# Eight attention units with output products of 32 columns and other PSUM banks, ahead of a two-layer product

## The chip, the cores and the metric

The kernel runs on one core of one Trainium2 chip. The metric is the device time of one execution in microseconds (us), the median of several runs. TensorE is called PE below, VectorE DVE, ScalarE ACT, GpSimd POOL; SP is the engine that issues all DMAs here. PSUM, the memory that PE writes to, has eight banks.

## The reference

```python
# q, k, v: (4, 8, 768, 64); mem_k, mem_v: (4, 8, 8, 64); chunk 32, left 16, right 8
for c in range(24):
    k_full = concat(mem_k, k[c*32 - 16 : c*32 + 40])      # clipped at both ends; v_full alike
    scores = q_c @ k_full.T / 8
    a = exp(scores - max); a = a / (sum(a) + 1e-9)
    out[c] = a @ v_full
x = out, as (3072 tokens, 512)
h = x @ w_in                                               # w_in (512, 2048)
g = max(h, 0) + alpha * min(h, 0)
result = g @ w_out                                         # w_out (2048, 512)
```

The weights w_in and w_out arrive as 8-byte floating point numbers and are turned into 4-byte ones on the chip ("decoded").

## The kernel before

The 3072 tokens make 8 blocks of 384. A block's attention is 4 units, each a pair of heads; unit u belongs to block u // 4. The two-layer product goes over 16 slices f of the hidden width: for block and slice, `up` forms h (12 products of 128x384), `sides` its two Relu (ACT, L581), `join` their sum with alpha (DVE), `high` and `low` split it in two parts, and `down` (9 products of 128x512) adds it onto the block's output in three banks o0 to o2 (L603). Such a step is written (block, f).

The first eight units (blocks 0 and 1) are computed by `windows`, before and among the first slices, while the weights still arrive. A unit u has these steps on PE, called s, t and v here, each with the unit's number behind it: s, 12 score products (L269), ahead of which 2 products of `busy` (8 for the first unit) go into the same bank; t, one such product and 3 transposes of the weights of attention (L435); v, 24 output products (L450). Between s and t DVE and ACT form the weights of attention (L407 to L428). Between t and v ACT copies the transposes to `et` (L440). After v `split` forms xh (ACT, L376) and xl (DVE, L380), the input of `up`. The scores of all eight units use bank s0, the transposes s1, the outputs bank a. Block 1's down products of the first nine slices use the same three banks s0, s1 and a; block 0's use o0 to o2.

The order of work is not that of the code. `Plan` collects steps with an engine, an estimated cost, what they read and write (names such as ("s", 0) stand for a bank), and a rank `rest`. `send` then goes through time by these estimates and lets each engine take, of the steps that could begin, the one with the most work behind it, or the highest `rest`. A step that writes a name waits for all that was planned before with that name. Each engine carries out its list in that order. SP too works its list in order, so a load that waits for its buffer holds up those behind it. The loads of values for units 4 to 7 (`vw`, L395) take over the buffers of units 0 to 3, and so wait for the v steps of those.

A matmul on 4-byte numbers (scores, outputs) shows in the profile as two matmul and two weight load records, one on the rounded numbers of `up` and `down` as one of each.

Of the kernel before, what the change touches and what calls it, by code (L numbers as in the profile page):

```python
# [9 lines left out]
F32 = mybir.dt.float32  # L10
# [8 lines left out]
P = 128  # L19
B, H, S, D = 4, 8, 768, 64  # L20
NM = 8
CH, LEFT, RIGHT = 32, 16, 8
# [12 lines left out]
NTT = BT // P  # L35
# [24 lines left out]
PE, DVE, ACT, POOL, SP = "PE", "DVE", "ACT", "POOL", "SP"  # L60
# [27 lines left out]
NWIN, NSET = 2 * NPAIR, 4  # L88
# [64 lines left out]
def body(ctx: ExitStack, tc: tile.TileContext, qvw, kw, vw, w_in, w_out, alpha, out):  # L153
# [15 lines left out]
    ps_o = ctx.enter_context(tc.tile_pool(name="ps_o", bufs=1, space=bass.MemoryType.PSUM))  # L169
    ps_s = ctx.enter_context(tc.tile_pool(name="ps_s", bufs=1, space=bass.MemoryType.PSUM))  # L170
    ps_a = ctx.enter_context(tc.tile_pool(name="ps_a", bufs=1, space=bass.MemoryType.PSUM))
# [12 lines left out]
    vws = [turned.tile([P, NT * NJ, D], F32, name=f"vw{i}", tag=f"pt{i}") for i in range(NPT)]  # L184
# [14 lines left out]
    step = plan.add  # L199
    state, xs = {}, {}  # L200

    def rest(place):
        return (len(ORDER) - place) * PAIR
# [8 lines left out]
    def due(u, later=0):  # L212

        return rest(begins(u) + later)
# [41 lines left out]
    def score_products(u):  # L256
        blk, pr = divmod(u, NPAIR)
        st = state[u]
        k = u % 2 if u >= NWIN else 0
        s_ps = ps_s.tile([P, 512], F32, name="s_ps", tag=f"s{k}")  # L260
        if u < NWIN:
            stir(s_ps, STIR[0] if u == 0 else STIR[1])
        st["s"] = s_ps[:, :NJ * 2 * KW].rearrange("p (n h k) -> p n h k", n=NJ, h=2)
        st["sg"] = s_ps[:, :NJ * 2 * KW].rearrange("p (n k) -> p n k", k=KW)
        for n in range(NJ):
            for g in range(4):
                t, j = SLOT[(g, n)]
                c = t * NJ + j
                nc.tensor.matmul(  # L269
                    out=st["s"][g * CH:(g + 1) * CH, n],  # L270
                    lhsT=qs[sets(u)][:, c * CH:(c + 1) * CH],
                    rhs=kbs[sets(u)][:, :, t, STARTS[j]:STARTS[j] + KW],
                    start=True, stop=True,
                )
# [90 lines left out]
             rest=due(u, DUE_VALUES))  # L365
        split(u)

    def split(u):

        st = state[u]  # L370

        slot = u % NX

        def high():
            st["xh"] = xp.tile([P, BT], F32R, name="xh", tag=f"xh{slot}")
            nc.scalar.copy(out=st["xh"], in_=st["a"][:, :BT])  # L376

        def low():
            xl = xp.tile([P, BT], F32R, name="xl", tag=f"xl{slot}")
            nc.vector.tensor_tensor(out=xl, in0=st["a"][:, :BT], in1=st["xh"].bitcast(F32), op=ALU.subtract)  # L380
            xs[u] = (st["xh"], xl)

        xh, xl = ("xh", slot), ("xl", slot)
        step(ACT, 0.48, high, reads=["a"], writes=[xh])
        step(DVE, 0.56, low, reads=["a", xh], writes=[xl])

    def vw_keys(u):
        i = u % NSET
        return [("pt", i, j) for j in range(len(TURNS))] if i < NPT else [("vw", i)]
# [9 lines left out]
    def windows(u):  # L399

        st = state[u]
        sk, tk = ("s", 0), ("s", 1)

        def top():
            hide(u)
            st["mx"] = sm.tile([P, NJ * 2, 1], F32, name="mx", tag=f"mx{u % 3}")
            nc.vector.tensor_reduce(out=st["mx"], in_=st["sg"], axis=AX.X, op=ALU.max)  # L407

        def less():
            st["e"] = at.tile([P, NJ * 2, KW], F32, name="e", tag=f"e{u % 2}")  # L410
            nc.vector.tensor_tensor(out=st["e"], in0=st["sg"], in1=st["mx"].broadcast_to([P, NJ * 2, KW]),  # L411
                                    op=ALU.subtract)

        def exps():
            nc.scalar.activation(out=st["e"], in_=st["e"], func=AF.Exp, scale=SCALE)

        def total():
            st["den"] = sm.tile([P, NJ * 2, 1], F32, name="den", tag=f"den{u % 3}")
            nc.vector.tensor_reduce(out=st["den"], in_=st["e"], axis=AX.X, op=ALU.add)

        def guard():
            nc.vector.tensor_scalar(out=st["den"], in0=st["den"], scalar1=1e-9, scalar2=None, op0=ALU.add)

        def inverse():
            nc.vector.reciprocal(out=st["den"], in_=st["den"])

        def scale():
            nc.vector.tensor_tensor(out=st["e"], in0=st["e"], in1=st["den"].broadcast_to([P, NJ * 2, KW]),  # L428
                                    op=ALU.mult)

        def turn():
            st["t"] = ps_s.tile([P, 512], F32, name="t_ps", tag="s1")
            stir(st["t"], STIR[2])
            for n in range(NJ):
                nc.tensor.transpose(st["t"][:, n * P:(n + 1) * P],  # L435
                                    st["e"][:, 2 * n:2 * n + 2].rearrange("p h k -> p (h k)"), eye)

        def keep():
            st["et"] = turned.tile([P, NJ, P], F32, name="et", tag="e2")
            nc.scalar.copy(out=st["et"].rearrange("p n q -> p (n q)"), in_=st["t"][:, :NJ * P])  # L440

        def values():
            st["a"] = ps_a.tile([P, 512], F32, name="a_ps", tag="a")
            for n in range(NJ):
                for g in range(4):
                    t, j = SLOT[(g, n)]
                    c = t * NJ + j
                    for h2 in range(2):
                        rows = slice(h2 * D, (h2 + 1) * D)
                        nc.tensor.matmul(  # L450
                            out=st["a"][rows, c * CH:(c + 1) * CH],
                            lhsT=vws[u % NSET][rows, c, :],
                            rhs=st["et"][rows, n, g * CH:(g + 1) * CH],
                            start=True, stop=True,
                        )

        step(PE, 0.82 + (0.44 if u < NWIN else 0), partial(score_products, u), reads=[("q", sets(u)), ("k", sets(u), 0), ("k", sets(u), 1)],
             writes=[sk], rest=due(u))
        step(DVE, 0.66, top, writes=[sk, ("mx", u % 3)])
        step(DVE, 0.52, less, reads=[sk, ("mx", u % 3)], writes=e_keys(u))  # L460
        step(ACT, 0.52, exps, writes=e_keys(u))
        step(DVE, 0.56, total, reads=e_keys(u), writes=den_keys(u))
        step(DVE, 0.16, guard, writes=den_keys(u))
        step(DVE, 0.19, inverse, writes=den_keys(u))
        step(DVE, 0.55, scale, reads=den_keys(u), writes=e_keys(u))
        step(PE, 0.68, turn, reads=e_keys(u) + ["eye"], writes=[tk], rest=due(u, 1))
        step(ACT, 0.48, keep, reads=[tk], writes=["e2"])
        step(PE, 1.55, values, reads=["e2"] + vw_keys(u), writes=["a"], rest=due(u, 1))
        split(u)

    def zero():

# [85 lines left out]
    def hidden(blk, f, first_f, last_f):  # L558
# [3 lines left out]
        place = PLACE[blk, f]  # L562
# [53 lines left out]
                     writes=[hk], rest=rest(place))  # L616

        def add_bend():
            step(ACT, 0.98, sides, reads=[hk], writes=[sd])
            step(DVE, 0.61, join, reads=["nal"], writes=[sd])  # L620
            step(*((ACT, 0.51) if place < HIGH_ACT else (DVE, 0.35)), high, reads=[sd], writes=[gh])
            step(DVE, 0.56, low, reads=[sd, gh], writes=[gl])

        def add_down(o_ps):
            step(PE, 2.09, partial(down, o_ps), reads=[("w", 1, f, 0), ("w", 1, f, 1), gh, gl],
                 writes=[("s", 0), ("s", 1), "a"] if joint else ["o"],
                 rest=rest(place + 1.5))

        return add_up, add_bend, add_down
# [13 lines left out]
    def store(blk, o_ps):  # L643
        def copy(tt, t, o):
            if blk == 1:
                o["t"] = kept[tt]
                nc.vector.tensor_tensor(out=o["t"], in0=o_ps[tt], in1=o["t"], op=ALU.add)
            else:
                o["t"] = tmp.tile([P, DM], F32, name="o_t", tag=f"o{t}")
                nc.scalar.copy(out=o["t"], in_=o_ps[tt])  # L650

        def send(tt, o):
            r = blk * BT + tt * P
            nc.sync.dma_start(out=out[r:r + P, :], in_=o["t"])

        for tt in range(NTT):
            t = tt if blk == 1 else NTT + tt % 2 if blk == 0 else next(ntmp) % NTMP
            o = {}
            place = PLACE[blk, NF - 1] + 1
            step(DVE if blk == 1 else ACT, 0.68 if blk == 1 else 0.59, partial(copy, tt, t, o), reads=["o"],  # L660
                 writes=[("tmp", t)], rest=rest(place))
            step(SP, 0.75, partial(send, tt, o), reads=[("tmp", t)])

# [115 lines left out]
```

## Time and profile before

| | |
|---|---|
| three runs | 629.96, 632.6 and 633.72 us, median 632.6 |
| profiled execution | 630.4 us, with a span from first to last instruction of 628.3 us |
| granted PE clock | 0.994 on average |
| PE, its weight loads, DVE, ACT, POOL busy | 615.9, 537.7, 402.7, 259.4, 25.7 us |
| moved by DMA | 48.43 MB in 22,596 packets |

Read it as three stretches. Up to about 50 us the units of blocks 0 and 1 are computed; DMA is full from 10 to 70 us (a share near 1.0), and the weights arrive. Until about 130 us weights are decoded on DVE and ACT beside the first slices. After that come blocks 2 to 7, with PE busy without a break until the last 4 us. All times of the trace count from the span's start.

### The profile page before, as it was taken

How to read it: one execution, taken by the hardware profiler on the slowest of the kernel's cores; microseconds unless marked ns; L12 is line 12 of the kernel's file. 1: busy time of each engine (PE TensorE's matmuls, PEld its weight loads, DVE VectorE, ACT ScalarE, POOL GpSimd, SP SyncE). 2: the span in 40 equal slices, each digit the busy share in tenths (PEclk: the TensorE clock that was granted, in tenths of full speed). 3: DMA queues.
4: the chain of work that ended last, by engine and by line, in shares of the span. 5: the costliest groups of instructions: out<-in, count | busy, mean ns of one | idle time of the engine just before them, and what ended most of it. 6: DMA issues, size and time to landing. Idle time of an engine off the chain costs nothing.

```text
span 628.3 us, 10982 instructions
## 1 busy us (share of the span) xinstructions
PE 615.9 (98%) x4278; PEld 537.7 (86%) x4278; DVE 402.7 (64%) x984; ACT 259.4 (41%) x716; POOL 25.7 (4%) x37
## 2 busy tenths in 40 slices
PE   6998999999999999999999999999999999999997
PEld 3687999988888889888888888898888888988996
DVE  6778898978747666477465765467563784633332
ACT  2387888765424243442324423144133433231212
POOL 1001000001000000000000000001000010000000
PEclk9898999999999999999999999999999999999999
DMA  8999700023222020320105001040012100010001
GB/s 236 301 404 409 245 1 2 0 62 97 66 62 68 21 69 23 98 79 2 47 18 158 18 18 36 30 142 18 18 49 79 50 18 18 18 51 1 1 1 50
DMA packets 22596, 48.43 MB, mean 77 GB/s; under 512 B 3088, under 2 KB 7184, under 8 KB 22544
## 3 DMA queue, kind: packets, MB, share of 16 engines
q1 hardware_dynamic: 22544, 47.73, 23.8%
q8 instruction: 33, 0.54, 0.4%
q14 instruction: 19, 0.16, 0.1%
HBM read 41.43 MB, written 6.29 MB: 76 GB/s over the span
## 4 chain that ended last, share of the span: by engine, by line
PE 93%; DMA 5%; SPq 1%; DVE 0%; ACT 0%; issue 0%
PE o_ps L603 43%; PE h_ps L571 42%; DMA w_t<-w_out 4%; PE s_ps L269 4%; PE a_ps L357 3%; PE a_ps L450 1%; DMA kb<-kw 1%; SPq L235 0%; PE s_ps L254 0%; DVE mx L407 0%; DVE e L411 0%; PE t_ps L435 0%; PE t_ps L254 0%; ACT o_t L650 0%; ACT dn L581 0%
## 5 line engine op out<-in xcount | busy, mean ns | idle before, releaser
L571 PE MATMUL h_ps<-xh,w 128*128 128x384 f32 x1024 | 262.6, 337 | 0.0
L603 PE MATMUL o_ps<-w,gh 128*128 128x512 f32 x768 | 239.8, 393 | 0.0
L571 PEld LDWEIGHTS h_ps<-xh,w 128*128 128x128 f32 x1024 | 186.8, 189 | 3.8
L571 PE MATMUL h_ps<-xl,w 128*128 128x384 f32 x512 | 174.7, 341 | 2.3 <-DVE xl L380 1.4
L581 ACT ACTIVATE up<-h_ps 128x384 f32<-128x384 f32 x128 | 63.4, 495 | 260.2 <-PE h_ps L571 253.3
L603 PEld LDWEIGHTS o_ps<-w,gh 128*128 128x128 f32 x768 | 144.1, 188 | 27.9
L603 PE MATMUL o_ps<-w,gl 128*128 128x512 f32 x384 | 153.1, 399 | 0.0
L585 DVE SCALAR_TENSOR_TENSOR up<-dn,nal,up 128x384 f32<-128x384 f32 x128 | 79.7, 627 | 113.3 <-ACT dn L581 112.5
L341 DVE STREAM_TRANSPOSE pt<-e 32x192 f32<-32x192 f32 (+1 forms) x336 | 99.5, 301 | 10.2 <-POOL e L320 4.6
L571 PEld LDWEIGHTS h_ps<-xl,w 128*128 128x128 f32 x512 | 96.7, 189 | 8.5 <-DVE xl L380 1.5
L603 PEld LDWEIGHTS o_ps<-w,gl 128*128 128x128 f32 x384 | 72.1, 188 | 16.9 <-issue 2.6
L595 DVE TENSOR_TENSOR gl<-up,gh 128x384 fp32r<-128x384 f32 x128 | 70.8, 557 | 3.2 <-ACT gh L591 0.5
L581 ACT ACTIVATE dn<-h_ps 128x384 f32<-128x384 f32 x128 | 62.3, 487 | 0.0
L299 ACT ACTIVATE e<-s_ps,mx 128x64 f32<-128x64 f32 x144 | 43.5, 323 | 29.3 <-DVE mx L293 28.4
L591 DVE CAST gh<-up 128x384 fp32r<-128x384 f32 x104 | 36.4, 355 | 20.5 <-PE o_ps L603 17.1
L320 POOL TENSOR_TENSOR e<-e,den 128x384 f32<-128x384 f32 x24 | 21.1, 878 | 465.4 <-DVE den L317 346.0
L299 ACT ACTIVATION_READ_ACCUMULATOR e<-s_ps,mx 128x1 f32 x144 | 30.7, 213 | 0.0
L376 ACT CAST xh<-a_ps 128x384 fp32r<-128x384 f32 x32 | 15.4, 481 | 34.3 <-PE a_ps L357 26.2
L269 PEld LDWEIGHTS s_ps<-kb,q 128*32 128x32 f32 x672 | 17.2, 111 | 8.1 <-issue 7.2
L269 PE MATMUL s_ps<-kb,q 128*32 128x128 f32 x672 | 23.6, 279 | 0.5 <-DMA kb<-kw 0.5
L357 PEld LDWEIGHTS a_ps<-pt,v_t 128*64 128x64 f32 x384 | 16.6, 136 | 7.4 <-issue 7.4
L357 PE MATMUL a_ps<-pt,v_t 128*64 128x96 f32 x384 | 21.1, 252 | 0.0
(59 smaller groups left out, 294.2 us busy)
## 6 DMA issues: line engine op xcount, KB each, us to landing
w_t<-w_in SPq DMA_DIRECT2D x16, 512.0 KB, 9.9
w_t<-w_out SPq DMA_DIRECT2D x16, 512.0 KB, 10.1
kb<-kw SPq DMA_DIRECT2D x56, 136.0 KB, 2.8
v_t<-qvw SPq DMA_DIRECT2D x24, 256.0 KB, 2.7
out<-o_t SPq DMA_DIRECT2D x24, 256.0 KB, 2.7
q<-qvw SPq DMA_DIRECT2D x28, 192.0 KB, 2.5
vw<-vw SPq DMA_DIRECT2D x4, 384.0 KB, 6.3
early<-vw SPq DMA_DIRECT2D x4, 384.0 KB, 7.1
```

What stands on the lines that cost most here:

```text
L269: nc.tensor.matmul(out=st["s"][g * CH:(g + 1) * CH, n], lhsT=qs[sets(u)][:, c * CH:(c + 1) * CH], rhs=kbs[sets(u)][:, :, t, STARTS[j]:STAR ...
L299: nc.scalar.activation(out=st["e"][:, i], in_=st["sg"][:, i], func=AF.Exp, scale=SCALE, bias=st["mx"][:, i:i + 1], accum_out=st["den"][:, i])
L320: nc.gpsimd.tensor_tensor(out=st["e"], in0=st["e"], in1=st["den"].broadcast_to([P, NJ * 2, KW]), op=ALU.mult)
L341: nc.vector.transpose(out=pts[u % NPT][quad * CH:(quad + 1) * CH, j, t0:t0 + n1 - n0].rearrange("p t h q -> p (t h) q"), in_=(st["e"], zer ...
L357: nc.tensor.matmul(out=st["a"][h2 * D:(h2 + 1) * D, t * TQ:(t + 1) * TQ], lhsT=st["v"][:, t, h2, :], rhs=pts[u % NPT][:, :, t, h2, :], sta ...
L376: nc.scalar.copy(out=st["xh"], in_=st["a"][:, :BT])
L571: nc.tensor.matmul(out=h["ps"][:, :BT], lhsT=ws[f, 0][:, wk, k * P:(k + 1) * P], rhs=xs[first + k][xk], start=(k == 0 and n == 0), stop=(k ...
L581: nc.scalar.activation(out=h[name], in_=h["ps"][:, :BT], func=AF.Relu, scale=sign)
L585: nc.vector.scalar_tensor_tensor(out=h["g"], in0=h["dn"], scalar=nal[:, f:f + 1], in1=h["up"], op0=ALU.mult, op1=ALU.add)
L591: copy(out=h["gh"], in_=h["g"])
L595: nc.vector.tensor_tensor(out=h["gl"], in0=h["g"], in1=h["gh"].bitcast(F32), op=ALU.subtract)
L603: nc.tensor.matmul(out=o_ps[tt], lhsT=h[gk][:, tt * P:(tt + 1) * P], rhs=ws[f, 1][:, wk], start=(f == first_f and i == 0), stop=(f == last ...
```

## The change

- A unit's 24 output products become 48: each gave 64 columns of the stationary operand, two of 32 columns now give the same output, placed on four strips of PSUM partitions, taken in the order strip 0, 2, 1, 3.
- The scores of the first eight units go in turn into s0 and s1. The transposes go into o0, the outputs into o1 and o2 in turn. So bank a is used by them no more, and the first down product of block 0 has to wait for the last unit's split. For this the planner's one name "o" becomes three.
- The planner's cost for the output products is 0.95 in place of 1.55.
- `sides` (the Relu) gets the rank of its up products.

```diff
     def score_products(u):
-        k = u % 2 if u >= NWIN else 0
+        k = u % 2
...
-    def split(u):
+    def split(u, ak="a"):
...
-        step(ACT, 0.48, high, reads=["a"], writes=[xh])
-        step(DVE, 0.56, low, reads=["a", xh], writes=[xl])
+        step(ACT, 0.48, high, reads=[ak], writes=[xh])
+        step(DVE, 0.56, low, reads=[ak, xh], writes=[xl])
...
     def windows(u):
-        sk, tk = ("s", 0), ("s", 1)
+        sk, tk, ak = ("s", u % 2), ("o", 0), ("o", 1 + u % 2)
...
-            st["t"] = ps_s.tile([P, 512], F32, name="t_ps", tag="s1")
+            st["t"] = ps_o.tile([P, 512], F32, name="t_ps", tag="o0")
...
-            st["a"] = ps_a.tile([P, 512], F32, name="a_ps", tag="a")
+            st["a"] = ps_o.tile([P, 512], F32, name="a_ps", tag=f"o{1 + u % 2}")
...
-                    for h2 in range(2):
+                    for h2, i in ((0, 0), (1, 0), (0, 1), (1, 1)):
                         rows = slice(h2 * D, (h2 + 1) * D)
                         nc.tensor.matmul(
-                            out=st["a"][rows, c * CH:(c + 1) * CH],
-                            lhsT=vws[u % NSET][rows, c, :],
+                            out=st["a"][h2 * D + i * CH:h2 * D + (i + 1) * CH, c * CH:(c + 1) * CH],
+                            lhsT=vws[u % NSET][rows, c, i * CH:(i + 1) * CH],
                             rhs=st["et"][rows, n, g * CH:(g + 1) * CH],
...
-        step(PE, 1.55, values, reads=["e2"] + vw_keys(u), writes=["a"], rest=due(u, 1))
-        split(u)
+        step(PE, 0.95, values, reads=["e2"] + vw_keys(u), writes=[ak], rest=due(u, 1))
+        split(u, ak)
...
-            step(ACT, 0.98, sides, reads=[hk], writes=[sd])
+            step(ACT, 0.98, sides, reads=[hk], writes=[sd], rest=rest(place))
...
-                 writes=[("s", 0), ("s", 1), "a"] if joint else ["o"],
+                 writes=[("s", 0), ("s", 1), "a"] if joint else [("o", tt) for tt in range(NTT)],
```

The instructions move on several engines. First PE, from the output products of unit 0 (`a_ps` with `vw_161`) on; `busy` rows are the products into a bank ahead of its use. Before:

```order
L450 MATMUL a_ps<-et,vw_161 64x32 x24
L254 LDWEIGHTS busy
L254 MATMUL t_ps<-busy 128x512
L435 MATMUL t_ps<-eye,e 128x128 x3
L254 LDWEIGHTS busy
L254 MATMUL s_ps<-busy 128x512
L254 LDWEIGHTS busy
L254 MATMUL s_ps<-busy 128x512
L269 MATMUL s_ps<-early 32x128 x12
L450 MATMUL a_ps<-et,vw_162 64x32 x24
```

and now:

```order
L450 MATMUL a_ps<-et,vw_161 32x32 x48
L254 LDWEIGHTS busy
L254 MATMUL t_ps<-busy 128x512
L435 MATMUL t_ps<-eye,e 128x128 x3
L450 MATMUL a_ps<-et,vw_162 32x32 x48
L254 LDWEIGHTS busy
L254 MATMUL s_ps<-busy 128x512
L254 LDWEIGHTS busy
L254 MATMUL s_ps<-busy 128x512
L269 MATMUL s_ps<-kb_154,q_159 32x128 x12
```

The scores of unit 3 (`early`) stood between t1 and v1; they now come ahead of t0, and v1 follows its transposes at once, ahead of the scores of unit 4. The order of the change is s0, s1, s2, s3, t0, v0, t1, v1, s4, t2, v2, s5, t3, v3, three up products' groups of (0, 0), s6, t4, s7, the last group of (0, 0), v4, t5, v5, three groups of (0, 1), t6, the last group of (0, 1), one of (1, 0), v6, t7, one of (1, 0), v7, where a group is three products.

Second PE, around the output products of unit 7 (`a_ps` with `early`) and the first down products (`o_ps`). Before:

```order
L571 MATMUL h_ps<-xh,w 128x384 x2
L603 MATMUL o_ps<-w,gl 128x512
L603 MATMUL o_ps<-w,gh 128x512 x2
L603 MATMUL o_ps<-w,gl 128x512
L603 MATMUL o_ps<-w,gh 128x512 x2
L603 MATMUL o_ps<-w,gl 128x512
L603 MATMUL o_ps<-w,gh 128x512 x2
L450 MATMUL a_ps<-et,early 64x32 x24
L571 MATMUL h_ps<-xl,w 128x384
```

and now:

```order
L571 MATMUL h_ps<-xh,w 128x384 x2
L450 MATMUL a_ps<-et,early 32x32 x48
L571 MATMUL h_ps<-xl,w 128x384
L571 MATMUL h_ps<-xh,w 128x384 x2
L571 MATMUL h_ps<-xl,w 128x384
L571 MATMUL h_ps<-xh,w 128x384 x2
L603 MATMUL o_ps<-w,gl 128x512
L603 MATMUL o_ps<-w,gh 128x512 x2
```

The nine down products of (0, 0) went ahead of v7; they now come after it, and after the last two groups of up products of (1, 0).

Third ACT, around the Relu of (1, 0) (`up`, `dn`) and the last step of decoding two weights (`w`). Before:

```order
L376 CAST xh<-a_ps 128x384
L537 CAST w<-a 128x512
L537 CAST w<-a 128x2x512
L581 ACTIVATE up<-h_ps 128x384
L581 ACTIVATE dn<-h_ps 128x384
L591 CAST gh<-up 128x384
```

and now:

```order
L521 COPY w_t<-w_t 128x512
L581 ACTIVATE up<-h_ps 128x384
L581 ACTIVATE dn<-h_ps 128x384
L537 CAST w<-a 128x2x512
L537 CAST w<-a 128x512
L591 CAST gh<-up 128x384 x2
```

Those two weights stood ahead of the Relu and now come behind it.

More of the change, by code (lines that the diff above doesn't have):

```diff
@@ L659, in store @@
             place = PLACE[blk, NF - 1] + 1
-            step(DVE if blk == 1 else ACT, 0.68 if blk == 1 else 0.59, partial(copy, tt, t, o), reads=["o"],
+            step(DVE if blk == 1 else ACT, 0.68 if blk == 1 else 0.59, partial(copy, tt, t, o), reads=[("o", i) for i in range(NTT)],
                  writes=[("tmp", t)], rest=rest(place))
```

## The prediction

> **What bounds the kernel now.** I read the page first, then busy time by stretch, then the waits of TensorE (PE).
>
> ```profile
> span 628.3 us, 10982 instructions
> ...
> PE 615.9 (98%) x4278; PEld 537.7 (86%) x4278; DVE 402.7 (64%) x984; ACT 259.4 (41%) x716; POOL 25.7 (4%) x37
> ...
> q8 instruction: 33, 0.54, 0.4%
> ```
>
> ```profile
> 0.00:50.57 50.57, 41.82 (x675) 30.83 (x675) 37.82 (x92) 25.86 (x47) 4.67 (x13) 0.97 0.99 320
> 50.57:628.30 577.73, 574.11 (x3603) 506.87 (x3603) 364.90 (x893) 233.59 (x670) 21.06 (x24) 1.00 0.18 56
> 600.00:628.30 28.30, 24.68 (x122) 21.75 (x120) 9.23 (x18) 6.73 (x15) 0.00 (x0) 0.98 0.08 28
> ```
>
> Columns: stretch, its length, then busy time and count of PE, its weight loads, DVE, ACT, POOL; granted clock; DMA share; GB/s. From 50.57 PE idles only in the 3.6 us of the end. So the end is 50.57 plus the PE work then left. The change adds nothing after the opening. It is worth what it does to the time at which PE becomes dense, and to what has been done by then.
>
> ```profile
> PE s_ps L254 <- DVE e L411: 2.9, 2, 1.4
> PE s_ps L254 <- DVE busy L176: 1.5, 1, 1.5
> PE h_ps L571 <- DVE xl L380: 1.4, 1, 1.4
> PE a_ps L450 <- issue: 1.0, 1, 1.0
> PE h_ps L571 <- ACT dn L581: 1.0, 1, 1.0
> PE a_ps L450 <- ACT et L440: 0.6, 1, 0.6
> PE s_ps L269 <- DMA kb<-kw: 0.5, 1, 0.5
> ```
>
> Of these 8.9 us the change aims at 2.9 (one bank for scores) and 1.0 (Relu late). The fourth line I take to be the one that decides. In PE's timeline:
>
> ```profile
> 23.72 0.88 PE L450 MATMUL a_ps<-et,early 64*64 64x32 f32 x23
> 25.60 0.94 PE L450 MATMUL a_ps<-et,early 64*64 64x32 f32 x25 [1.00 <-issue]
> ```
>
> One group of 48 output products stops after 23 and goes on 1.0 us later, with no wait inside the group. PE's instructions come in by queue q8: 33 packets of 16 KB for 2 x 4278 matmuls and loads, 259 each. Since 33 packets carry nearly the whole program, little of it is held ahead. Below, the stretches end where one of these packets starts, but for the second, which ends at the stall; then two answers on the packets themselves, each for 0.02 us that holds the start of one, at 22.89 and at 31.04.
>
> ```profile
> 0.00:22.89 22.89, 17.54 (x298) 11.11 (x298) 15.48 (x41) 7.37 (x15) 2.89 (x10) 1.00 0.93 265
> 0.00:25.50 25.50, 19.25 (x345) 12.47 (x345) 18.05 (x49) 8.34 (x16) 2.89 (x10) 1.00 0.94 264
> 25.50:31.04 5.54, 5.44 (x93) 3.95 (x95) 3.52 (x9) 1.95 (x4) 0.00 (x0) 0.69 1.06 281
> 31.04:37.07 6.03, 6.03 (x107) 5.08 (x104) 4.79 (x15) 4.57 (x8) 0.00 (x0) 1.00 1.03 401
> 37.07:43.04 5.97, 5.90 (x75) 5.24 (x74) 5.97 (x14) 4.49 (x8) 0.00 (x0) 1.00 1.03 408
> 43.04:63.27 20.23, 17.89 (x123) 15.96 (x122) 16.11 (x23) 16.52 (x25) 1.78 (x3) 0.92 1.03 408
> 84.69:109.27 24.58, 24.58 (x124) 22.13 (x123) 21.81 (x29) 21.30 (x29) 0.00 (x0) 1.00 0.00 1
> 109.27:130.78 21.51, 21.51 (x129) 19.17 (x128) 18.63 (x27) 15.95 (x31) 0.00 (x0) 1.00 0.06 18
> ```
>
> ```profile
> q8 instruction: 1, 0.02, 366.6%
> ```
>
> ```profile
> q8 instruction: 1, 0.02, 332.8%
> ```
>
> Late in the run a packet starts every 247 or 257 instructions: one for each block used up. In the opening the gap is not PE's pace but the packets': the DMA engines are full (share 1.03 to 1.06). The packet at 22.89 takes 366.6% of 16 engines' 0.02 us, 1.17 us, and ends at 24.06; PE goes on at 25.60, 1.54 us later. If the next is asked for when PE enters the new block, 25.60, its packet starts 5.44 us after, takes 1.06 and is usable 1.54 later, at 33.6. By the same steps the following ones are usable at 39.7 and 45.6. So **a block of about 256 instructions costs 8.0, 6.0 or 6.0 us, on average 6.7**, when DMA is full. PE hides this now because it uses only 188 to 211 instructions per packet in 25.5 to 37.07.
>
> [...]
>
> **The parts.**
>
> *Products of 32 columns.* 24 matmuls of a unit become 48; each is two records, so 48 matmuls and 48 loads become 96 and 96.
>
> ```profile
> 16.94 1.59 PE L450 MATMUL a_ps<-et,vw 64*64 64x32 f32 x48
> ...
> 8.64 0.16 PEld L269 LDWEIGHTS s_ps<-kb,q 128*32 128x32 f32 x8 [0.42 <-issue]
> 8.64 0.32 PE L269 MATMUL s_ps<-kb,q 128*32 128x128 f32 x4
> ```
>
> The 48 run as 24 pairs in 1.59 us, 66 ns a pair. Afterwards they are 24 groups of four, on four column strips. The score products (a look at 8.60 to 8.70) start 8 loads of 32 columns and 4 matmuls within 0.06 us, so four strips go side by side. If a group's pace follows the columns loaded, 64 to 32, it halves: about 24 x 33 ns, plus a tail, 0.9 us. From above: if a pair costs what it costs now and nothing goes side by side, 3.2 us. I take 0.9, nearest to the score row: **-0.65 us x 8 = -5.2 us** of PE work, unless instructions are late. [...]
>
> *Instructions.* The 8 units gain 8 x 96 = 768, three blocks, all in the opening. Counting matmuls and loads in the new order: before the eighth unit ends there are 16 (first stir), 8 x 48 scores, 7 x 4 stirs, 8 x 8 transposes with stir, 8 x 192 products, and 30 up products with their loads, 2088. The old order stalls at 690. From there, block limits stand at 946, 1202, 1458, 1714 and 1970: inside v2 (the third unit's products) at 690, in v3, at the end of t4, of t5, in v6 and in v7. Block [690, 946) is asked for as now when PE enters the one before it, in v1, near 17 to 18.6 us as in the old order; usable at 25.6. PE's work between two limits is at most 5.2 us (block from 1458: 0.9 for v5, 10 up products in three groups 1.7, transposes, copy), below 6.7, so each limit is a stall: usable at 32.3, 39.0, 45.7, 52.4, **59.1**. The last 118 instructions of v7 take 0.6 us: 59.7.
>
> *Scores in two banks.* s2 and s3 (scores of the third and fourth unit) now come ahead of the first transposes, which move behind keys that must land:
>
> ```profile
> 12.26 0.39 PE L254 MATMUL t_ps<-busy 128*128 128x512 bf16 x1
> ...
> 16.15 0.86 PE L269 MATMUL s_ps<-early 128*32 128x128 f32 x24
> ```
>
> From 12.26 the transposes go to at most 17, after s3 where it ran before. That costs nothing as long as v2 is reached before 25.6: from 17 on come t0, v0, t1, v1, s4 and t2, with copies 6 us. Without the stall it would be part of the second rival's bill.
>
> *Where PE then stands.*
>
> ```profile
> 45.85 1.59 PE L450 MATMUL a_ps<-et,early 64*64 64x32 f32 x48
> 48.82 0.44 PE L571 MATMUL h_ps<-xl,w 128*128 128x384 f32 x1 [1.38 <-DVE xl L380]
> 50.57 0.69 PE L571 MATMUL h_ps<-xl,w 128*128 128x384 f32 x1 [0.96 <-ACT dn L581]
> ...
> 57.44 0.39 PE L603 MATMUL o_ps<-w,gl 128*128 128x512 f32 x1
> 58.12 0.39 PE L603 MATMUL o_ps<-w,gl 128*128 128x512 f32 x1
> ...
> 60.54 0.33 PE L571 MATMUL h_ps<-xl,w 128*128 128x384 f32 x1
> 61.06 0.33 PE L571 MATMUL h_ps<-xl,w 128*128 128x384 f32 x1
> ```
>
> Now: at 50.57, 36 up and 9 down products are done. Then: at 59.7, 30 up and no down product, since the first downs share the banks of the windows' outputs and wait for the last split. Three up products take 0.52, three down 0.68 us: 6 x 0.173 + 9 x 0.227 = 3.1 us behind. After v7 comes the split of unit 7, now 1.4 us, of which one up group (0.5) hides a part: +0.9; behind the waiting downs PE's queue holds the up products of the next slices, which wait with them. Sum: 59.7 + 0.9 + 3.1 - 50.57 = **+13.1 us**. It holds the 0.6 us a unit saved, the two score waits and the Relu's 0.96 us (all before 50.57) as already given back. The half-speed clock costs the same on both sides: 0.92 over 20.2 us now, 1.6 us, after idling near 48; afterwards 1.6 us after the stall before 59.1.
>
> *Loads.* The value loads of units 4 to 7 wait for the products of units 0 to 3; v3 ends near 34.5 instead of 26.5, and SP holds the weights behind them.
>
> ```profile
> 30.16 0.33 SPq L395 DMA_DIRECT2D early<-vw  x1
> ```
>
> That load would go 4 to 5 us later, and the weights after it. At 408 GB/s the 1 MB of one slice comes in 2.6 us, while PE needs 8.4 us for a slice (12 up, 9 down, two blocks). So 5 us late costs nothing, with PE late by 9. *Relu's rank* puts (1, 0)'s Relu ahead of two weight casts on ACT, the 0.96 us above; after 50.57 PE waits for ACT nowhere, and with PE late the casts have more lead than now: nothing.
>
> **Sum.** The profiled run took 630.4 us for a span of 628.3; 630.4 + 13.1 = 643.5. The median shown, 632.6, is 2.2 higher, so I say **644.5**. Bounds: 6.0 us a block gives 5 x 0.7 less, +9.6, 640; 8.0 gives 5 x 1.35 more, +20, 650 to 652.5.
>
> **Rivals.**
>
> *Fetch costs little, gain stays* (0.20). If a request reaches the DMA engines early, or runs further ahead than one block, what is left is 2.6 us (1.06 + 1.54) a block, which PE hides. Then -5.2 of products, -2.9 of score waits, -1.0 of Relu, -1.0 of the stall; back comes 0.57 us for the copy between transposes and products, which stand next to each other now, in 6 units, +3.4: -6.7, 624. For it: three of the four packets after the stall came in time. Against it: the stall, at a lower rate of instructions.
>
> *Near no change* (0.09): requests cost about 5 us a block, as less DMA is queued while SP waits. The last stall then ends at 25.6 + 5 x 5 = 50.6, +4.6 us, less up to 4 if the first stall shortens as well: 630 to 635.
>
> *The products get slower* (0.04): 2.4 to 3.2 us a unit, from the point where 96 pairs start more than 16 ns apart (1.59 us). [...]
>
> The forecast keeps 0.67. A measurement of this kernel tells about 0.5%, 3 us, from no change: faster by more 0.19 (the gain, but for 0.01), within 0.10, slower by more 0.71. The forecast's own range is 637 to 655. For 8 in 10 I reach down into the near-equal case and the upper part of the gain: **627 to 655**.
>
> **What would show it.** Right: L450 groups of 96 broken by "issue" waits of 2 to 5 us, at five or six places, each ending about 1.5 us after a q8 packet's end; 36 packets; v7 ending near 60; an unbroken group near 0.9 us; first down products after the last L450; granted clock below 1 in several stretches up to 60 us. Wrong: q8 packets 3 us apart in the opening, or stalls at other counts than 256 apart; an unbroken group over 1.6 us; PE idle after 65 us, which would say that the Relu's rank or the late weights cost what I put at nothing.

## The result and the profile after

The change makes the kernel slower: 640.84 us as the median of 4 runs (639.46 to 641.09), against 633.16 us for the kernel before (4 runs, 629.96 to 635.19). The ratio is 1.0149, with a 95% interval from 1.0112 to 1.0185. The profiled run took 640.67 us for a span of 638.9. That is 10.3 us more than the profiled run before, where the medians say 7.7: the profiled run before, 630.4 us, lies low beside its four. The forecast was 644.5.

The page of the change, its span, its first section and PE's instruction queue:

```profile
span 638.9 us, 11769 instructions
...
PE 616.9 (97%) x4662; PEld 534.4 (84%) x4662; DVE 400.9 (63%) x984; ACT 260.3 (41%) x716; POOL 26.6 (4%) x37
...
q8 instruction: 36, 0.59, 0.4%
```

There are 384 more matmuls, 384 more loads and three more packets. PE's busy time grew by 1.0 us only, and the span by 10.6, so nearly all that was lost is idle time. PE's waits in the first 62 us (what it waited for; us in total, times, longest) say which:

```profile
PE a_ps L450 <- issue: 8.7, 5, 3.6
PE a_ps L450 <- ACT et L440: 2.4, 4, 0.6
PE a_ps L450 <- DMA vw<-vw: 1.9, 1, 1.9
PE t_ps L435 <- issue: 1.6, 1, 1.6
...
PE s_ps L269 <- DMA early<-kw: 1.4, 2, 0.8
PE s_ps L269 <- DMA kb<-kw: 0.9, 1, 0.9
```

The two "issue" lines are 10.3 us; before it was one wait of 1.0. The rest changed names and not size. Gone are 2.9 us for a free bank of scores, 1.4 for `xl` and 1.0 for the Relu, together 5.3. New are 1.8 more for the copy `et`, 1.9 for values and 1.8 more for keys, together 5.5.

PE's timeline shows where the waits for instructions stand (start, duration, count; in brackets the idle time ahead):

```profile
18.09 0.98 PE L450 MATMUL a_ps<-et,vw 64*32 64x32 f32 x92 [0.54 <-issue]
25.35 1.19 PE L450 MATMUL a_ps<-et,early 64*32 64x32 f32 x91 [1.86 <-issue]
32.62 1.40 PE L450 MATMUL a_ps<-et,early 64*32 64x32 f32 x90 [1.96 <-issue]
40.53 1.02 PE L450 MATMUL a_ps<-et,vw 64*32 64x32 f32 x96
41.49 0.39 PE L254 MATMUL t_ps<-busy 128*128 128x512 bf16 x1
43.43 0.55 PE L435 MATMUL t_ps<-eye,e 128*128 128x128 f32 x3 [1.56 <-issue]
...
56.34 0.94 PE L450 MATMUL a_ps<-et,early 64*32 64x32 f32 x63 [3.61 <-issue]
59.57 0.60 PE L603 MATMUL o_ps<-w,gl 128*128 128x512 f32 x1
61.84 0.33 PE L571 MATMUL h_ps<-xl,w 128*128 128x384 f32 x1
```

One more, of 0.72 us, ends at 50.04. Five of the six breaks lie inside a group of 96 matmul records (the 48 output products of a unit, two records each), the sixth in the transposes of t5. The first group that no break cuts starts at 40.53, and the next instruction at 41.49: 0.96 us for 96 records, where the 48 records of the wider products took 1.52 (16.94 to 18.46 before). The edit on the products did what it says, 0.57 us a unit.

That the breaks are limits of instruction blocks is seen by counting what PE has begun when it goes on. Columns as in the prediction's windows:

```profile
0.00:25.30 25.30, 16.16 (x345) 8.67 (x346) 15.74 (x43) 6.95 (x13) 2.89 (x10) 0.93 0.90 247
0.00:32.60 32.60, 20.84 (x472) 11.44 (x473) 19.17 (x53) 9.49 (x18) 2.89 (x10) 0.90 0.93 265
0.00:43.40 43.40, 30.10 (x727) 18.56 (x727) 23.91 (x65) 12.41 (x24) 2.89 (x10) 0.88 0.91 274
...
0.00:56.30 56.30, 37.96 (x981) 24.91 (x982) 32.40 (x85) 21.19 (x39) 2.89 (x10) 0.91 0.94 305
0.00:61.84 61.84, 43.46 (x1060) 29.51 (x1060) 36.32 (x92) 25.68 (x46) 4.67 (x13) 0.89 0.95 314
```

The matmuls and loads begun by then are 691, 945, 1454 and 1963: 254 apart, then 509 twice, and between the last two lies the break at 50.04. The limit near 1200 was passed without a stall. The windows leave out the records of PE's queue that only wait for a semaphore or drain, 12 to 22 by then. With these the six breaks of the trace stand behind 449, 705, 961, 1473, 1729 and 1985 records: 256 or 512 apart.

Each restart follows a q8 packet. This answer holds 0.02 us at the start of the packet at 47.72:

```profile
q8 instruction: 1, 0.02, 345.3%
```

In 16 engines' time (0.32 us per 100%) that is 1.10 us. With starts and shares from further such answers, the six packets behind the stalls end at 16.48, 23.91, 31.22, 41.98, 48.83 and 54.92; PE goes on 1.61, 1.44, 1.39, 1.45, 1.21 and 1.42 us after that. How long PE waited for a packet to start is seen in two stretches, each from a restart to the start of the next packet:

```profile
43.43:47.72 4.29, 3.66 (x111) 3.05 (x112) 3.24 (x10) 3.38 (x6) 0.00 (x0) 1.00 1.02 415
32.62:34.09 1.47, 1.47 (x91) 1.41 (x90) 0.00 (x0) 0.04 (x1) 0.00 (x0) 0.53 0.81 323
```

With the DMA engines full it is 4.29 us (4.53, 4.80 and 3.78 from 18.09, 25.35 and 50.04). In the second row, where SP waited for v3 and the DMA share fell to 0.81, it is 1.47, and that block was the one that came in time. Full DMA engines do not give one number, though: at shares of 1.0 and more the distance is 2.2 us at one place and 5.4 at another, as the kernel before shows (further below).

The account at the same work: before, 36 up and 9 down products were done at 50.57; now at 61.84, 11.3 us later. PE's idle time up to there is 61.84 - 43.46 = 18.4 us, before 50.57 - 41.82 = 8.75: 9.6 more, and the instruction waits grew by 9.3. Busy time grew by 1.6 despite 4.5 us saved on products, mainly since four stretches of 3.41 us ran at a clock of 0.5 (from 19.05, 25.87, 32.70 and 56.59), and before only one by then (from 26.67). After it the kernel before still has such a stretch to pay, from 50.56. The mean clock does not explain the loss: the four runs of the change had a mean granted clock of 0.984 to 0.989, and the 18 runs of the kernel before that are on record with 0.984 to 0.988 took 633.0 us in the median, 7.8 less than the change.

### The profile page after: what moved, and what is told of

Read it like the earlier page. It is cut to its first block, busy times and chain, and to the rows that moved or that the text cites. A ratio compares the mean times of both kernels' runs of the same rounds, so it can differ in the third digit from the quotient of the medians.

```text
span 638.9 us, 11769 instructions
## 1 busy us (share of the span) xinstructions
PE 616.9 (97%) x4662; PEld 534.4 (84%) x4662; DVE 400.9 (63%) x984; ACT 260.3 (41%) x716; POOL 26.6 (4%) x37
## 4 chain that ended last, share of the span: by engine, by line
PE 94%; issue 2%; DMA 1%; SPq 1%; DVE 1%; ACT 0%; ACTq 0%
PE h_ps L571 43%; PE o_ps L603 43%; PE s_ps L269 4%; PE a_ps L357 3%; PE a_ps L450 1%; DMA vw<-vw 1%; SPq L235 1%; SPq L232 0%; PE s_ps L254 0%; PE t_ps L435 0%; ACT et L440 0%; PE t_ps L254 0%; DVE mx L407 0%; ACT o_t L650 0%; SPq L395 0%
## 5 line engine op out<-in xcount | busy, mean ns | idle before, releaser
L269 PEld LDWEIGHTS s_ps<-kb,q 128*32 128x32 f32 x672 | 17.7, 114 | 10.3 <-issue 7.5
L269 PE MATMUL s_ps<-kb,q 128*32 128x128 f32 x672 | 25.4, 288 | 0.9 <-DMA kb<-kw 0.9
L380 DVE TENSOR_TENSOR xl<-a_ps,xh 128x384 fp32r<-128x384 f32 x32 | 17.7, 553 | 9.0 <-ACT xh L376 9.0
```

The lines of the kernel that those rows point to most:

```text
L269: nc.tensor.matmul(out=st["s"][g * CH:(g + 1) * CH, n], lhsT=qs[sets(u)][:, c * CH:(c + 1) * CH], rhs=kbs[sets(u)][:, :, t, STARTS[j]:STAR ...
```

## The experiments

The theory to test: **PE's instructions are late**, because 768 more records pass in an opening whose DMA engines are full, at some 6 us a block of 256. The rivals: the new order of the units (scores in two banks, transposes next to products) costs it; the Relu's rank or the late weights cost it; the 32-column products themselves cost it.

**One part undone: 64 columns.** The change with the output products as before.

```diff
-                    for h2, i in ((0, 0), (1, 0), (0, 1), (1, 1)):
+                    for h2 in range(2):
                         rows = slice(h2 * D, (h2 + 1) * D)
...
-        step(PE, 0.95, values, ...
+        step(PE, 1.55, values, ...
```

> The change with its output products put back to 64 columns (24 a unit, cost 1.55 in the planner); banks, orders by turn and the Relu's rank stay. Late instructions as the cause: 768 fewer records, so the stalls ahead of 256-instruction limits shrink to the one or two of the kernel before; 628 to 632 us, 33 q8 packets, no wait by issue over 2 us. Rival, banks and order as the cause (transposes and outputs next to each other, first down product behind the last split): 638 us or more with few waits by issue.

Measured 630.29 us (12 runs) against 630.25 (23 runs), ratio 0.9997 (0.9975 to 1.0019). There are 33 packets, and no wait for instructions among PE's waits. The longest of these:

```profile
PE s_ps L269 <- DMA early<-kw: 3.1, 2, 2.1
```

So all that the change loses hangs on the columns, and the two banks, the Relu's rank and the order that the planner makes with them are together worth nothing. That order is not the change's everywhere: with the cost at 1.55 the scores of unit 4 stand between t1 and v1 again. And in the profiled run the granted clock was 0.50 from 13.40 to 23.60, so the one wait of 1.0 us of the kernel before may be missing because PE came to that limit late. The 2.9 us for a bank of scores went, and 3.1 us for keys (`kw`) stand in their place: scores that no longer wait for a bank wait for their load.

**One part alone: 32 columns.** The kernel before, with only the loop over columns changed; the planner's cost and so the order stay.

```diff
-                    for h2 in range(2):
+                    for h2, i in ((0, 0), (1, 0), (0, 1), (1, 1)):
                         rows = slice(h2 * D, (h2 + 1) * D)
                         nc.tensor.matmul(
-                            out=st["a"][rows, c * CH:(c + 1) * CH],
-                            lhsT=vws[u % NSET][rows, c, :],
+                            out=st["a"][h2 * D + i * CH:h2 * D + (i + 1) * CH, c * CH:(c + 1) * CH],
+                            lhsT=vws[u % NSET][rows, c, i * CH:(i + 1) * CH],
```

> The kernel before with only the output products in 32 columns; order, banks and planner costs as before. Late instructions: five or six stalls every 256 instructions from the 449th or 705th on, 36 q8 packets, last one near 55 us; 638 to 645 us. Rival, banks and order: no loss, 5 us of products saved, 625 to 633 us.

Measured 643.29 us, ratio 1.0175 (1.0134 to 1.0215): the whole loss. First two of its waits, then one of its five breaks in the timeline:

```profile
PE a_ps L450 <- issue: 10.5, 5, 3.9
PE s_ps L254 <- DVE e L411: 2.9, 2, 1.4
```

```profile
20.35 0.26 PE L450 MATMUL a_ps<-et,early 64*32 64x32 f32 x6
24.55 1.49 PE L450 MATMUL a_ps<-et,early 64*32 64x32 f32 x90 [3.94 <-issue]
```

By the same count its breaks lie at 438, 692, 946, 1200 and 1709 records begun; with the waiting records it is 449, 705, 961, 1217 and 1729, the counts of the change in another order of work. From its five restarts to the start of the next packet it is 4.27, 3.54, 2.33, 3.58 and 3.73 us, at DMA shares of 1.03 to 1.07. The score waits of before are still there, so this order is not what the change lost by. These two runs settle which part costs.

**The Relu's rank alone.** The kernel before with one argument.

```diff
-            step(ACT, 0.98, sides, reads=[hk], writes=[sd])
+            step(ACT, 0.98, sides, reads=[hk], writes=[sd], rest=rest(place))
```

> The kernel before with only the Relu's rank changed. Late instructions as the cause: this part costs nothing; the 0.96 us wait for the Relu goes, 631 to 633.5 us. Rival, the rank delays the decoding of weights: PE idle for ACT or DVE between 55 and 130 us, 635 us or more.

Measured 630.44 us, ratio 0.9988 (0.9963 to 1.0014). The wait for `dn` is gone, and PE waits at the same up products for weights that are decoded later:

```profile
PE h_ps L571 <- DVE w L540: 0.9, 1, 0.9
```

1.0 us was traded for 0.9.

**Records without the columns.** If the count of instructions costs, 48 idle matmuls a unit must cost the same 768 records in the kernel before. First with one column, in bf16, into unread columns of the bank:

```diff
+            for i in range(48):
+                h2, j = i % 2, i // 2 % 2
+                nc.tensor.matmul(out=st["a"][h2 * D + j * CH:h2 * D + (j + 1) * CH, BT:BT + 1],
+                                 lhsT=busy[h2 * D:(h2 + 1) * D, :CH], rhs=busy[h2 * D:(h2 + 1) * D, :1],
+                                 start=True, stop=True)
```

> [...] Late instructions: the same stalls as the change, 636 to 645 us. [...]

Measured 646.45 us, ratio 1.0227 (1.0185 to 1.027), and no wait for instructions at all. As an instrument it failed. Its timeline:

```profile
21.48 1.51 PE L269 MATMUL s_ps<-early 128*32 128x128 f32 x24
22.92 2.77 PE L450 MATMUL a_ps<-et,vw 64*64 64x32 f32 x48
...
51.86 0.86 PE L269 MATMUL s_ps<-early 128*32 128x128 f32 x24
```

The scores take 1.51 us up to 50 us and 0.86 after it, the products 2.77 instead of 1.59: PE ran at half speed through the opening. The idle matmuls themselves took 0.45 us a unit (25.62 to 26.07). I take it that at that pace a block lasts long enough to be fetched in time, and that the half speed is the loss, which is another cause than the one under test. It says nothing for or against the theory.

The second attempt has 128 columns in each idle matmul (`BT:BT + 128`, `:128`).

> [...] 768 more records. Late instructions: waits by issue of 8 to 11 us in total at records 256 apart, as with 32 columns alone; the small ones' own work is about 0.65 us a unit (four in 54 ns); 638 to 648 us. Rival, number of instructions is not the cause: no wait by issue over 1.2 us, and at most that own work, 633 to 637 us, unless the clock stays at half again.

Measured 643.96 us, ratio 1.019 (1.0144 to 1.0236). In its timeline, a group of the idle matmuls and the first break:

```profile
23.26 0.85 PE L458 MATMUL a_ps<-busy 64*32 64x128 bf16 x48
25.91 0.41 PE L450 MATMUL a_ps<-et,early 64*64 64x32 f32 x6
27.46 1.47 PE L450 MATMUL a_ps<-et,early 64*64 64x32 f32 x42 [1.13 <-issue]
```

The breaks come back in products that are as wide as before: after 6 of their records here, at a count of 689, and one unit later after 7, at 942, with 2.6 us. The sum of the waits is 4.3 us, half of what I expected. The scores ahead of both breaks take 0.86 us (25.12 and 30.71), so PE was not at half speed there. The idle matmuls take 0.79 us a unit, where I had 0.65, 6.3 us in all, and this time covers part of the fetches. So the count alone brings the waits, shown at two places; the run doesn't give the price cleanly.

**A shorter queue ahead of a packet: loads in quarters.** Each weight load of 512 KB becomes four of 128 KB, in the change and in the kernel before. From 39.13 to 50.64 the kernel before issues whole loads 1.28 us apart, each after SP has waited for an earlier one to land, and a load lands 10 us after its issue (medians 9.9 and 10.1): by these numbers about eight are under way, 4 MB. How many quarters are, no run shows.

```diff
-            nc.sync.dma_start(out=raw[k][:, j].rearrange("p m b -> p (m b)"), in_=srcs[i][f])
+            for c in range(0, P, P // 4):
+                nc.sync.dma_start(out=raw[k][c:c + P // 4, j].rearrange("p m b -> p (m b)"), in_=srcs[i][f, c:c + P // 4])
```

> The change with each weight load of 512 KB issued as four of 128 KB, so that the eight loads that may be under way hold 1 MB instead of 4 MB. If instruction packets are late because they queue behind weight loads, a block costs 4 to 5 us instead of 6.2, the last stall ends near 47 to 51 us instead of 56.3, and the time is 632 to 637 us. Rival, a block has a price of its own that the queue does not set: same stalls, 639 to 642 us.

> The same splitting in the kernel before. It has one stall of 1.0 us to lose: 628 to 631 us by both theories, unless 128 KB pieces carry the weights more slowly, which would show in PE waiting for decoded weights and 633 us or more.

Measured 636.15 us for the change (ratio to the kernel before 1.0076, 1.0046 to 1.0107) and 634.2 for the kernel before (1.0047, 1.0015 to 1.0079). The waits of the changed kernel with quarters, then a stretch of it:

```profile
PE a_ps L450 <- issue: 3.7, 3, 1.3
...
PE t_ps L435 <- issue: 2.6, 2, 2.4
...
PE s_ps L254 <- issue: 0.7, 2, 0.3
```

```profile
40.00:50.00 10.00, 8.94 (x254) 7.57 (x255) 6.50 (x17) 7.37 (x14) 0.00 (x0) 0.83 0.92 226
```

The instruction waits fall from 10.3 to 7.0 us, the last one ends at 51.07 instead of 56.34, and a block costs (51.07 - 24.55) / 5 = 5.3 us instead of (56.34 - 25.35) / 5 = 6.2. What the change costs over its own control falls to 1.95 us. PE's order of work is the same, so part of the price is set by how the transfers share the DMA engines; 7.0 us of waits remain. It is no way out: the quarters move 226 GB/s where whole loads moved 415, and make the kernel before slower as well.

**No weights at all in the opening.** Slices 2 to 12 are not loaded; GpSimd writes zeros in their place, so these kernels leave those weights out of the result.

```diff
-            nc.sync.dma_start(out=raw[k][:, j].rearrange("p m b -> p (m b)"), in_=srcs[i][f])
+            if 2 <= f < NF - 3:
+                nc.gpsimd.memset(raw[k][:, j], 0)
+            else:
+                nc.sync.dma_start(out=raw[k][:, j].rearrange("p m b -> p (m b)"), in_=srcs[i][f])
```

> The change without the weight loads of slices 2 to 12: GpSimd sets those weights to zero. From about 25 us on DMA is nearly idle. Late packets behind the loads: the stalls from the 961st instruction on shrink to below 1 us or go, a block costs 3 to 5 us, the last output products end before 50 us; span 10 us or more below the change's 638.9. Rival, the price of a block is its own, or lies in order and banks: stalls of 2 to 3.6 us stay, span 636 to 640.

> The kernel before without the weight loads of slices 2 to 12, for comparison: no wait by issue, span 625 to 629. Late packets: the change without those loads is then no more than 3 us slower than this, or faster. Rival: it stays 8 to 12 us slower.

Measured once each, 642.97 us in the change and 644.32 in the kernel before. Both are spoiled: GpSimd wrote zeros from 3.62 to 23.33, and a VectorE operation on 128x6 elements that takes 0.17 us elsewhere in this trace took 13.80, from 9.56 to 23.36; PE waited for it. One line each, the change first:

```profile
PE t_ps L435 <- DVE den L422: 12.7, 1, 12.7
```

```profile
PE s_ps L254 <- DVE e L411: 17.1, 2, 15.7
```

The instruction waits fell to 2.9 us, as the theory wants, but a PE that stands 12.7 us behind another engine gives packets time to come. Inconclusive.

**Weights paced.** So I let the loads be, and held those of slices 3 to 6 until the outputs `xh` of units 4 to 7 were cast, by a copy of one element on GpSimd, in both kernels.

```diff
+    GATES = {3: 4, 4: 5, 5: 6, 6: 7}
...
+                nc.gpsimd.tensor_copy(out=raw[f, 0].bitcast(F32)[:1, j, 0, :1], in_=state[u]["xh"].bitcast(F32)[:1, :1])
...
-    for f in range(NF - 3):
+    for f in range(min(GATES)):
         load_w(f)
     for u in range(NWIN):
         unit_begins(u)
+    for f in range(min(GATES), NF - 3):
+        load_w(f)
```

> The change with the weight loads of slices 3 to 6 held back until the outputs of units 4 to 7 are there (GpSimd copies one element of xh into the buffer first), and those of later slices behind them; PE's order up to the first down products is the change's. Packets late behind weight loads: the stalls at the 1473rd, 1729th and 1985th record shrink to below 1 us, the last output products end at 46 to 51 us instead of 57, 630 to 636 us. Rival, a block's price is its own: the same stalls, 639 us or more.

> The same holding back in the kernel before. Packets late behind weight loads: nothing to win but the one stall, which lies ahead of the held loads: 629 to 633 us. If the weights then come too late, PE waits for decoded weights near 55 us and it takes 634 us or more. If this and the change held back come out alike, the saved 5 us of products went into what stalls are left.

Measured 637.67 us for the change, ratio 1.0101 (1.0067 to 1.0136), and 631.25 for the kernel before, ratio 1.0004 (0.9975 to 1.0033). The pacing costs the kernel before nothing, so what the change loses over this control is 6.4 us. That is more than the 630 to 636 us that I expected, and the waits for instructions add up to 10.0 us, hardly less than the change's 10.3. Two limits in the middle pass without a wait, but there are 2.3 us at 19.06, where the change has 0.5, and 2.3 at 36.81, where it has none. So the sum does not show the theory; single stretches do. The changed kernel passes through a full and an empty stretch of DMA:

```profile
28.40:34.33 5.93, 4.57 (x133) 3.54 (x134) 3.48 (x11) 1.88 (x4) 0.00 (x0) 1.00 1.01 375
36.81:38.53 1.72, 1.72 (x15) 0.81 (x19) 1.29 (x3) 1.00 (x2) 0.00 (x0) 0.54 0.07 29
38.53:42.49 3.96, 3.70 (x123) 2.61 (x115) 1.99 (x6) 1.60 (x4) 0.00 (x0) 0.77 0.01 4
```

```profile
36.81 0.40 PE L435 MATMUL t_ps<-eye,e 128*128 128x128 f32 x1 [2.33 <-issue]
40.56 1.02 PE L450 MATMUL a_ps<-et,vw 64*32 64x32 f32 x96
42.85 1.02 PE L450 MATMUL a_ps<-et,vw 64*32 64x32 f32 x96 [0.62 <-ACT et L440]
47.30 1.02 PE L450 MATMUL a_ps<-et,early 64*32 64x32 f32 x96
...
53.33 0.74 PE L450 MATMUL a_ps<-et,early 64*32 64x32 f32 x63 [3.14 <-issue]
```

After the restart at 36.81 the next packet starts within 1.72 us, at a DMA share of 0.07, and takes 0.92 us; with 1.4 for the restart such a block costs 4.0 us. Three whole groups of 96 (40.56, 42.85, 47.30) then run unbroken, past the two limits that follow 254 and 508 records after that restart. When the held loads come together (329 GB/s in 45 to 50), the next limit stalls for 3.1 us. Within one run the same kernel stalls with DMA full and doesn't with DMA empty. The clock in the empty stretch was low too (0.54 and 0.77 in the rows above), so PE asked for less there; but how soon the packet starts, 1.72 us after the restart against 4.29 in the change, does not hang on that. This is the clearest sign for the theory's second half.

**The rest of the way: half the units, weights held to unit 7.** The 32 columns only in units 4 to 7, where the held weights leave the DMA engines free.

```diff
+                    w = CH if u >= 4 else D
-                    for h2, i in ((0, 0), (1, 0), (0, 1), (1, 1)):
+                    for h2, i in ((0, 0), (1, 0), (0, 1), (1, 1))[:2 * D // w]:
...
+    GATES = {f: 7 for f in range(3, NF - 3)}
```

> The change with 32 columns only in units 4 to 7 (64 in units 0 to 3, so 384 records fewer than the change, 384 more than before), and the weights of slice 3 and later held back until the outputs of unit 7. While DMA is light a block should cost near 4 us, as after 34 us in the change held back: one or two waits by issue of under 2 us, last output products by 47 us, 627 to 632 us, so no slower than before and perhaps up to 0.5% faster. Rival, late instructions cost by their number whatever DMA does: half the change's loss, 634 to 637 us. If the weights come too late, PE waits for decoded weights after 50 us.

Measured 634.02 us, ratio 1.0053 (1.0024 to 1.0082), above the range I gave and at the edge of the rival's 634 to 637, so the time does not decide between the two. The waits for keys of the 64-column run came back, and two limits still broke, one of them for 2.4 us:

```profile
PE s_ps L269 <- DMA early<-kw: 3.1, 2, 2.5
PE a_ps L451 <- issue: 2.8, 2, 2.4
```

The break of 2.4 us ends at 42.37. Two groups of 96 had run nearly back to back from 37.45, with DMA full until 39 (share 0.99 in 38 to 39, 0.70 in 39 to 40). After that restart, with a share of 0.00, the next packet starts within 1.26 us (43.63), and no limit broke again. No version found beats the kernel before.

## Why the prediction was right

**The mechanism held.** The waits are for instructions, they come with the count (2 x 384 records, three packets more), they go when the columns are undone (630.29), they come with the columns alone (643.29), and they shrink when the transfers beside them change (7.0 us with quarters; none past two limits with DMA empty, though that run's sum stayed at 10.0). The rival that fetches are hidden gave 624, the one of equal time 630 to 635; neither fits an interval that begins at 1.0112.

**The price of a block was a little too high on average, and this is the term that was mis-sized.** I took 6.7 us, the mean of 8.0, 6.0 and 6.0, for every block alike. Measured is 6.2: the last stall ended at 56.34 and not 59.1, which is 2.8 us, as much as lies between +13.1 and the +10.3 measured in the profile; the smaller errors below cancel. The blocks are not alike: from stall to stall it is 7.3 us (25.35 to 32.62), then 10.8 for the two blocks around the limit that did not stall, 6.6 and 6.3. My lower bound of 6.0 a block, 640, is closer to the median than my forecast.

**That 6.7 came so close is partly luck.** The two figures of 6.0 are distances between packets in the kernel before, read as what a block costs. By the prediction's own assumption, that a packet is asked for when PE enters the block ahead of it, they are not that. Behind the stall at 691, limits 254 apart put PE's entries at 34.75 (944 records begun) and 40.84 (1199). It did not have to wait at either, and the packets started 2.32 and 2.20 us later, with DMA full:

```profile
34.75:37.07 2.32, 2.32 (x74) 2.08 (x74) 1.36 (x4) 1.40 (x4) 0.00 (x0) 1.00 1.02 403
40.84:43.04 2.20, 2.20 (x14) 1.97 (x14) 2.20 (x5) 2.15 (x4) 0.00 (x0) 1.00 1.03 410
```

With 1.06 and 1.54 us behind it that is 4.9 and 4.8 us a block, the price of the rival of near no change. The 8.0 came from one wait of 5.44 us. In the change the packets then started 3.5 to 4.8 us after a restart with DMA full, so the forecast's price was nearly right for a reason that it did not have. What makes the same full DMA cost 2.2 us at one place and 4.8 at another, no run here shows.

**Places.** The first break, where the old order already stalled, came at 691 records and PE went on at 25.35; I had 690 and 25.6. Of the five that I put behind it four came, within 7 of the counts given (I had counted 256 without the waiting records). The limit near 1200 was missed: its packet started 1.47 us after the restart, as SP held back loads behind v3 and PE ran at half speed from 32.70. I had seen that SP would wait, had priced it as late weights (nothing, rightly), and had not asked what an emptier queue does for the packets. A small break of 0.54 us at 18.09, one block earlier, I had not foreseen.

**Products.** 0.96 us a group against 0.9 forecast. The rival of slower products is out by this: the products became faster, and four strips do run side by side, four records in 40 ns where two took 63 before (48 in 1.52 us). No run shows the 2.4 us a unit that the rival begins with; 96 records in 0.96 us are 10 ns each, and 20 ns a product. Its 3.2, the pace of before with nothing side by side, would give 630.4 - 6.7 + 8 x 2.3 = 642 us, so it is the products that speak against it and not the time.

**What stands behind the last stall.** I had 0.6 for the end of v7, 0.9 of waiting for the split of unit 7, and 3.1 for products behind. The split cost nothing, since two groups of up products stood between v7 and the first down product (57.20 to 59.57), not one. Six up and nine down products took 57.20 to 61.84, 4.64 us; 2.8 us of the half-speed stretch from 56.59 lie there and cost 1.4, so 3.2. The kernel before has the same stretch of clock after 50.57, as I had said, so 1.7 of the 11.3 us at equal work should come back; of that 0.7 does (577.73 us left before, 577.06 now), and where the other 1.0 went I have not found. Ahead of the last stall, three half-speed stretches (5.1 us of PE time lost) stand against one (1.7) before, which I had put at no difference. Where PE waits for packets anyway, such a loss should stand in the place of a wait; that is argued, and fits that the change's four runs do not follow their clock (639.46 us at 0.984, 640.67 at 0.989).

**The score banks and the Relu** had been put at nothing under the stall. The runs say more: they are worth nothing without the stall too (630.29 and 630.44), and waits for key loads (3.1 us) and for weights (0.9 us) of that size appear in their places. In the hidden-fetch rival I had counted 3.9 us as gain from them. That would have been wrong, and 624 with it.

**Open.** The request for a block is taken to be made when PE enters the block before; the packets' times fit that, but no row shows a request. How much of a wait of 4.3 us is the transfers' queue and how much a fixed part is bounded only by the 1.72 and 1.26 us at DMA shares of 0.07 and 0.00. No run shows the opening without weights in flight and unspoiled.

## What to carry to other kernels

Before you cut matmuls into more and smaller ones, count the records per microsecond: a block of 256 instructions cost 6 to 7 us behind a stall here while loads filled the DMA engines (6.2 on average in the change), and about 4 us beside light ones (4.0 in the paced run), so a stretch that used more than one block in that time waited for its own program. Look for "issue" waits inside a group of like instructions, and whether the counts at which they fall are equally far apart. And when a wait goes, run that part alone: twice here the next wait in line was as long as the one removed.

## What the runs showed of the hardware that I had not expected

**Half-speed stretches differ from run to run and are worth microseconds.** The profiled run of the kernel before with paced weights has none:

```profile
0.00:48.50 48.50, 39.39 (x669) 29.86 (x675) 37.67 (x92) 25.79 (x47) 7.72 (x21) 1.00 0.85 275
```

It took 626.52 us, the lowest of 12 runs of that kernel (626.5 to 634.4). The kernel before had two stretches of 3.41 us at 0.50 and took 630.4. Each costs at most 1.7 us, so two explain most of the 3.9. The mean granted clock is on record for 73 runs of the kernel before, and the time goes with it: 18 runs with 0.984 to 0.988 took 632.59 to 635.73 us, 12 with 0.996 to 0.999 took 626.64 to 629.28. That it is stretches of this kind in those runs too is not shown, as only profiled runs show where the clock was low.

**With one-column matmuls PE ran at half speed.** With 48 of them a unit, durations were doubled for the first 51 us, while the granted clock of that stretch was printed as 1.00:

```profile
0.00:52.00 52.00, 46.93 (x711) 32.90 (x715) 25.44 (x67) 14.05 (x26) 2.90 (x10) 1.00 0.86 271
```

The durations of known instructions are the better witness of the clock: 1.51 us for 24 score records, where full speed gives 0.86, and where the change takes 1.50 in its stretch with a granted clock of 0.50 (27.43).
